# Moving the big loads of a decode kernel from SyncE's queue to GpSimd's, each as one packet

## The chip, the cores and the metric

The kernel runs on one core of one Trainium2 chip. The time is the device time of the program in microseconds (us), the median of several runs. Besides TensorE (PE), VectorE (DVE), ScalarE (ACT), GpSimd (POOL) and SyncE (SP), the core has 16 DMA engines, which move data between the chip's memory (HBM) and the on-chip memory SBUF. An engine that issues a DMA only hands it over; the 16 DMA engines do the moving, and a semaphore is raised by 16 when all of them are done.

## The reference

One step of decoding: attention over a cache of keys and values, beside a small MLP, on 8 batch rows. All arrays are bf16.

```
xn  = layernorm(x)                                  # x [8, 1, 640]
q   = (layernorm(x) @ wq) as [8, 32 heads, 1, 128]
p   = softmax(q . k_cache * 128**-0.5)              # k_cache [8, 32, 4096, 128]
o   = p . v_cache                                   # v_cache [8, 32, 4096, 128]
out = x + o @ wo + (gelu(layernorm(xn) @ w1 + b1) @ w2 + b2)   # w1 [640, 1728]
```

Each of the two caches has 8 x 32 x 4096 x 128 elements of two bytes, 268 MB. Every element is used once. Together with the weights 552 MB are read.

## The kernel before

**Tiles.** The work on the cache is cut into 32 rounds (`NQ`), one for a group of eight heads of one batch row. A round's keys are 8 heads x 4096 keys x 128 elements. They lie as 128 partitions of 256 keys (`NKEY`), that is 128 rows of 64 KB, 8192 KB in all; 16 partitions hold one head. The values of a round have the same layout. SBUF has three slots of this size: KA and KB take the keys of even and odd rounds, VS the values. There is no room for a fourth, so a load waits until its slot has been read for the last time.

**A round.** Scores are made in two ways at once. Of a partition's 256 keys, 80 go through TensorE: it transposes them eight keys at a time (`pe_T`), ScalarE copies the transposes from PSUM to SBUF (`act_T`), TensorE multiplies them with the queries (`pe_QK`). The other 176 go through DVE in three chunks (`dve_chunk`): a multiply with the query, which writes into the key slot itself, an addition of the two halves, a sum. `dve_sel` folds TensorE's part to the head that a partition holds, `dve_max` finds the maximum, `act_exp` makes the probabilities, `pe_PV` runs 256 small matmuls over the values, and `pe_RS`, `dve_rinv`, `act_O` and `o_norm` divide by the sum. GpSimd's own work in a round is small: `qrep` repeats the query, `k_ready` writes one number when the keys have landed and so releases TensorE, `o_norm` multiplies 128 x 8 numbers.

**Order.** The kernel writes one list of steps with positions (`at(position, function, ...)`) and sorts it; round i stands at 100 i. Each step appends instructions to its engine's list, with waits for tickets (a semaphore and a count). An engine does its own list strictly in order. TensorE's, DVE's and ScalarE's lists are then folded into hardware loops (`_replay_pe`, `_replay_loop`); those of SP and GpSimd are written out in full (`_replay`).

**Loads.** SP issues nearly all of them, in this order: wq (into the value slot), K0, K1, V0, then K(i+1) and V(i) by turns, the MLP weights, V31, Wo. `load_k` (line 365) waits, for rounds 2 to 5, for the last transposes and the last DVE chunk of round i-2 (tickets `kt`, `km`), and from round 6 on for the exp of round i-2; `load_v` (line 380) waits for the `pe_PV` of round i-1 (ticket `pv`). The value load of round 30 is cut in two DMAs at key 192 (`V_CUT`, line 240), so that `pe_PV(30)` can begin with the first piece; in TensorE's loop the second piece's semaphore is counted by an extra one (`_late`), which `consts_pool` raises first.

**The end.** After K31 the key slot KA is free for w1, w2 and what is made of them (`load_mlp`, line 375; `zero_w2b`, `load_w2b`; `sel_pool`, two large copies by GpSimd; `widen`, line 517, eight small ones that wait for w1 and b1). b1 comes through ACT's queue (`load_b1`), behind ScalarE's copy of round 30's result. When the keys of round 31 have been read, Wo comes into KB (`load_wl`, `load_wn`, lines 396 and 403), and the last matmuls use it while it arrives in pieces.

Of the kernel before, what the change touches and what calls it, by code (L numbers as in the profile page):

```python
# [14 lines left out]
P = 128  # L15
# [177 lines left out]
def bass_parallel_sum__gqa_block_cached__mixer_channel_mlp__decode_kernel(  # L193
# [21 lines left out]
    NQ = NHQ * B  # L215
    DC = D // P
    FB = F // P
# [11 lines left out]
    NS = 2  # L229
    LOOP0, LOOPN = 2, 15  # L230
    KLATE = 6
    assert NKEY == 256 and NQ == 32
    SLOT = NKEY * DH
    KA, KB, VS = 0, 1, 2
# [1 line left out]
    RW = P // HW  # L236
    NL = 3
    WN_CUT = (0, 5 * CT, 7 * CT, 7 * CT + CT // 2, HS * CT)
    V_CUT = (0, 192, 256)

    def jp_of(i):
        return 80
# [6 lines left out]
    def kslot(i):  # L249
        return KA if i % 2 == 0 else KB  # L250
# [8 lines left out]
    with ExitStack() as es:  # L259
        sb = lambda name, shape, dt: es.enter_context(nc.sbuf_tensor(name, shape, dt))  # L260
        ps = lambda name, shape, dt: es.enter_context(nc.psum_tensor(name, shape, dt))
        sem = lambda name: es.enter_context(nc.semaphore(name))

        S_sb = sb("S_sb", [P, 3, SLOT], BF)
        tile = [S_sb[:, s, :].rearrange("p (j d) -> p j d", d=DH) for s in range(3)]
# [12 lines left out]
        w1_sb = scratch(DC * F, P, KA).rearrange("p (c n) -> p c n", c=DC)  # L278
        w2_sb = scratch(FB * D, P, KA).rearrange("p (c n) -> p c n", n=D)
# [69 lines left out]
        ld_vl = [_Dma(sem(f"ld_vl{q}")) for q in range(1, len(V_CUT) - 1)]  # L349
        ld_wl = [_Dma(sem(f"ld_wl{q}")) for q in range(2)]  # L350
        ld_wn = [_Dma(sem(f"ld_wn{q}")) for q in range(len(WN_CUT) - 1)]
        tk = {}
        prog = []

        def at(pos, fn, *a):
            prog.append((pos, len(prog), fn, a))

        def load(key, dma, dst, src, eng=None):
            tk[key] = dma.sig((eng or sp).dma_start(dst, src))

        def cache_src(cache, i):
            hq, b = divmod(i, B)
            return cache[b, hq * HS:(hq + 1) * HS].rearrange("h (p j) d -> (h p) j d", j=NKEY)

        def load_k(i):
            s = kslot(i)
            if i >= KLATE:
                sp.wait(tk[("exp", i - 2)])
            elif i >= 2:
                sp.wait(tk[("kt", i - 2)], tk[("km", i - 2)])  # L370
            elif s == KB:
                sp.wait(tk["qmm"])
            tk[("k", i)] = ld_s[s].sig(sp.dma_start(tile[s], cache_src(A_k_cache, i)))

        def load_mlp():
            sp.wait(tk[("kt", NQ - 2)], tk[("km", NQ - 2)])
            load("w1", ld_w1, w1_sb, B_w1.rearrange("(p c) f -> p c f", c=DC))
            load("w2a", ld_w2a, w2_sb, B_w2[0:FB * P, :].rearrange("(p c) n -> p c n", c=FB))
# [12 lines left out]

        def load_b1():
            act.wait(tk[("kt", NQ - 2)], tk[("km", NQ - 2)])
            load("b1", ld_b1, b1_sb, B_b1.rearrange("(o f) -> o f", o=1), act)

        def load_wl(q):
            sp.wait(tk[("kt", NQ - 1)], tk[("km", NQ - 1)])
            lo, hi = (0, HW) if q == 0 else (HW, HW + HS)
            tk[("wl", q)] = ld_wl[q].sig(sp.dma_start(
                woW_sb if q == 0 else woL_sb[:, 0, :],  # L400
                A_wo[lo * DH:hi * DH, :].rearrange("(p s) n -> p (s n)", p=P)))

        def load_wn(q):
            lo, hi = WN_CUT[q], WN_CUT[q + 1]
            n = HS * DH
            tk[("wn", q)] = ld_wn[q].sig(sp.dma_start(
                woL_sb[:, 1, lo * CN:hi * CN],
                A_wo[NL * n:(NL + 1) * n, :].rearrange("(p s) n -> p (s n)", p=P)[:, lo * CN:hi * CN]))

# [12 lines left out]
        def consts_pool():  # L422
            pool.iota(iota_h, [[-HP, HS]], base=0, channel_multiplier=1)
            pool.iota(iota_w, [[-RW, HW]], base=0, channel_multiplier=1)
            tk["iota"] = pool.sig(pool.iota(iota_i, [[1, P]], base=0, channel_multiplier=-1))
            for d, (ap, v) in zip([None] + ld_vl + [None] * 2, (
                    (zeros_sb, 0.0), (ones_sb[:, :], 1.0), (mx_sb[:, :], 0.0), (mb_sb[:, :], 0.0))):
                inst = pool.memset(ap, v)
                if d is not None:
                    inst.call[3] = (d.sem, 1)  # L430
            tk["consts"] = pool.sig(pool.memset(ones_f[:, :], 1.0))

        def sel_pool():
# [186 lines left out]
        def dve_chunk(i, c):  # L620
            s = i % 2
            lo, hi = chunks(i)[c]
            w = hi - lo
            kt = tile[kslot(i)][:, lo:hi, :]
            dve.wait(tk[("k", i)], tk[("qb", i)])
            t = dve.sig(dve.tensor_tensor(
                kt, kt, qbc_sb[:, s, :][:, None, :].to_broadcast([P, w, DH]), ALU.mult))
            tk[("ym", i)] = t
            dve.wait(t)
            t = dve.sig(dve.tensor_tensor(kt[:, :, 0:DH // 2], kt[:, :, 0:DH // 2], kt[:, :, DH // 2:DH], ALU.add))  # L630
            dve.wait(t, tk.get(("exp", i - 2)))
            tk[("km", i)] = dve.sig(dve.tensor_reduce(Sd_sb[:, s, lo:hi], kt[:, :, 0:DH // 2], AX.X, ALU.add))
# [311 lines left out]
```

## Time and profile before

| | us |
|---|---|
| median of 3 runs | 1281.46 (1281.36 to 1281.47) |
| span of the profiled execution | 1280.1 |
| DVE busy | 1101.6 (86%) |
| PE busy | 672.0 (52%) |
| ACT busy | 477.0 (37%) |
| POOL busy | 109.3 (9%) |
| DMA queue q1 (SP's) | 551.79 MB in 10736 packets, 99.7% of 16 engines' span |
| other queues | q8 and q14 (instructions) 13 packets, q10 (ACT's) 36 packets |

The span reaches from the first to the last instruction; the run's time has a little more around it. A DMA queue's share is the time that its packets took, summed over the 16 DMA engines and divided by 16 spans. "Us to landing" of an issue counts from the issuing instruction to the last semaphore update, so it holds the time that the load waited behind others. Nearly every instruction has line L111, the helper that emits it, so groups are told apart by tiles: `S_sb` is the three slots, `kr_sb` the number that `k_ready` writes, `PV_ps` the result of `pe_PV`. In a timeline a row gives the start, the duration, the engine (a q behind it: issue only), the operation, the tiles and the count; brackets give the idle time of the engine before it and what ended it. "issue" there means that the profile shows nothing it waited for.

### The profile page before, as it was taken

To read this page: it belongs to the slowest core of one execution; us is meant where nothing else is said; L and a number is where in the kernel's file an instruction comes from. 1 tells how busy PE (TensorE), PEld (TensorE's weight loads), DVE (VectorE), ACT (ScalarE), POOL (GpSimd) and SP (SyncE) were. 2 spreads that over 40 slices of the span, in tenths; PEclk is the share of its full clock that TensorE was granted. 3 is DMA by queue.
4 is the path that set the end of the run, shared out by engine and by line. 5 is a ranking of instruction groups with operands and counts; after the bars stand their busy time and mean duration, and the time that the engine had idled before them with its cause. 6 is when DMAs were issued, how large, how long until landed. Compare 5 with 4: busy or idle time off the path is not lost.

```text
span 1280.1 us, 34355 instructions
## 1 busy us (share of the span) xinstructions
PE 672.0 (52%) x13906; PEld 573.2 (45%) x13906; DVE 1101.6 (86%) x681; ACT 477.0 (37%) x906; POOL 109.3 (9%) x119
## 2 busy tenths in 40 slices
PE   1636555446645446545456554456454466464476
PEld 1435444335535345444345444345343355353465
DVE  1899999889888889888898888898888898888894
ACT  0524444233444233443234443234442334442331
POOL 0020010000000000000000000000000000000050
PEclk9755565565565556555555555556555656655665
DMA  9999999999999999999999999999999999999998
GB/s 419 427 433 431 432 430 432 442 432 430 430 442 428 432 432 436 436 430 432 432 442 430 430 432 438 432 430 434 436 436 430 432 430 442 432 428 434 432 440 367
DMA packets 10785, 551.99 MB, mean 431 GB/s; under 512 B 1242, under 2 KB 1523, under 8 KB 1812
## 3 DMA queue, kind: packets, MB, share of 16 engines
q1 hardware_dynamic: 10736, 551.79, 99.7%
q8 instruction: 9, 0.15, 0.0%
q10 hardware_dynamic: 36, 0.02, 0.0%
q14 instruction: 4, 0.03, 0.0%
HBM read 551.80 MB, written 0.01 MB: 431 GB/s over the span
## 4 chain that ended last, share of the span: by engine, by line
DMA 47%; DVE 37%; issue 11%; ACT 4%; DVEq 0%; SPq 0%; PE 0%
DMA S_sb<-in_A_k_cache_dram 45%; DVE S_sb L111 26%; DVE Sd_sb L111 8%; ACT P_sb L111 4%; DMA S_sb<-in_A_wo_dram 2%; DVE S_ps L111 1%; DVE mx_sb L111 1%; DVE mbT_sb L111 0%; DVE mxT_sb L111 0%; DVE ri_sb L111 0%; DVE NB_sb L111 0%; DVEq L109 0%; DVE mq_sb L111 0%; DVE mb_sb L111 0%; SPq L111 0%
## 5 line engine op out<-in xcount | busy, mean ns | idle before, releaser
L111 PE MATMUL TR_ps<-ident_bf,S_sb 128*128 128x128 bf16 (+1 forms) x2570 | 343.3, 280 | 353.5 <-POOL kr_sb L111 333.2
L111 DVE TENSOR_TENSOR S_sb<-S_sb,qbc_sb 128x7552 bf16<-128x7552 bf16 (+1 forms) x96 | 388.7, 4049 | 128.3 <-DMA S_sb<-in_A_k_cache_dram 128.0
L111 PEld LDWEIGHTS TR_ps<-ident_bf,S_sb 128*128 (+2 forms) x2570 | 245.7, 103 | 411.7 <-issue 338.5
L111 DVE TENSOR_REDUCE Sd_sb<-S_sb 128x59 f32<-128x3776 bf16 (+1 forms) x96 | 390.2, 4065 | 6.0
L111 ACT ACTIVATE KT_sb<-TR_ps 128x1024 bf16<-128x1024 bf16 x320 | 327.0, 1024 | 121.6 <-PE TR_ps L111 109.6
L111 PE MATMUL PV_ps<-P_sb,S_sb 128*128 128x8 bf16 x8192 | 224.0, 175 | 140.6 <-DMA S_sb<-in_A_v_cache_dram 137.9
L111 PEld LDWEIGHTS PV_ps<-P_sb,S_sb 128*128 128x128 bf16 x8192 | 221.3, 103 | 143.3 <-DMA S_sb<-in_A_v_cache_dram 140.5
L111 DVE TENSOR_TENSOR S_sb<-S_sb 128x3776 bf16<-128x3776 bf16 (+1 forms) x96 | 206.5, 2151 | 3.3
L111 ACT ACTIVATE P_sb<-Sd_sb,NB_sb 128x256 bf16<-128x256 f32 x256 | 126.3, 494 | 210.9 <-DVE NB_sb L111 210.9
L111 PE MATMUL S_ps<-qrep_sb,KT_sb 128*128 128x8 bf16 x2560 | 121.9, 177 | 50.9 <-ACT KT_sb L111 47.8
L111 ACT ACTIVATE oU_sb<-PV_ps 128x8 f32<-128x8 f32 x31 | 5.5, 178 | 375.8 <-PE PV_ps L111 375.8
L111 PEld LDWEIGHTS S_ps<-qrep_sb,KT_sb 128*128 128x128 bf16 x2560 | 91.7, 103 | 82.4 <-ACT KT_sb L111 41.1
L111 POOL TENSOR_TENSOR oT_sb<-oU_sb,ri_sb 128x8 bf16<-128x8 f32 x31 | 71.8, 2315 | 370.8 <-DVE S_sb L111 315.3
L111 POOL COPY qrep_sb<-qT_sb 128x128 bf16<-128x128 bf16 x32 | 18.3, 573 | 474.7 <-PE S_ps L111 455.1
L111 ACT ACTIVATION_READ_ACCUMULATOR P_sb<-Sd_sb,NB_sb 128x1 f32 x256 | 47.8, 187 | 0.0
L111 DVE TENSOR_TENSOR S_ps<-S_ps,mask_sb 128x320 f32<-128x320 f32 (+1 forms) x65 | 31.6, 486 | 2.7 <-PE S_ps L111 2.7
L111 DVE TENSOR_REDUCE Sd_sb<-S_ps 128x40 f32<-128x320 f32 x64 | 31.5, 492 | 2.2
L111 PE MATMUL QB_ps<-ident_bf,qrep_sb 128*128 128x128 bf16 x32 | 9.1, 285 | 40.7 <-DVE S_sb L111 22.1
L111 ACT ACTIVATE qbc_sb<-QB_ps 128x128 bf16<-128x128 f32 x32 | 8.9, 278 | 57.6 <-PE QB_ps L111 57.6
L111 POOL MEMSET kr_sb<- 128x1 f32 x32 | 3.2, 99 | 294.9 <-DMA S_sb<-in_A_k_cache_dram 294.9
L111 PEld LDWEIGHTS QB_ps<-ident_bf,qrep_sb 128*128 128x128 bf16 x32 | 3.3, 103 | 43.6 <-ACT oU_sb L111 29.0
L111 PE MATMUL CH_ps<-rs_sb,ones_f 128*128 128x8 f32 x64 | 15.4, 313 | 6.5 <-ACT P_sb L111 6.5
(68 smaller groups left out, 150.6 us busy)
## 6 DMA issues: line engine op xcount, KB each, us to landing
S_sb<-in_A_v_cache_dram SPq DMA_DIRECT2D x1, 6144.0 KB, 26.8
S_sb<-in_A_wq_dram SPq DMA_DIRECT2D x1, 5120.0 KB, 15.6
S_sb<-in_A_wo_dram SPq DMA_DIRECT2D x1, 2560.0 KB, 18.4
S_sb<-in_B_w_dram SPq DMA_DIRECT2D x1, 2160.0 KB, 30.3
S_sb<-in_B_w_dram SPq DMA_DIRECT2D x1, 2080.0 KB, 34.9
S_sb<-in_A_v_cache_dram SPq DMA_DIRECT2D x1, 2048.0 KB, 31.4
S_sb<-in_A_wo_dram SPq DMA_DIRECT2D x1, 1280.0 KB, 21.1
S_sb<-in_A_wo_dram SPq DMA_DIRECT2D x1, 800.0 KB, 22.6
```

Of the source, the lines that this page charges most:

```text
L111: inst = getattr(e, name)(*a, **k)
```

## The change

- K2 to K31 and all V loads, the MLP weights w1 and w2 (except w2's last rows) and all of Wo are issued by GpSimd. wq, K0, K1 and w2's last rows stay with SP. GpSimd's list holds the issues between its other steps, so an issue also stands behind those.
- Each of these K and V loads has `single_packet`: the eight rows that a DMA engine moves for it are one packet instead of eight.
- V30 is one DMA: `V_CUT` has no inner cut, so `ld_vl` is empty and the extra counts go.
- The loads by GpSimd have semaphores of their own (`ld_g`).
- V0 waits, besides for the query matmuls, for the multiply of DVE's second chunk of round 0 (`ym0`).
- In the list, K(i) from round 2 on stands right behind `k_ready(i-1)` (100 i - 101) instead of behind `qrep(i)` (100 i - 51), and `load_mlp` just ahead of `k_ready(31)`. The tickets that they wait for are the same.

```diff
+    PACKET = {"single_packet": True}
...
-    V_CUT = (0, 192, 256)
+    V_CUT = (0, 256)
...
+        ld_g = [_Dma(sem(f"ld_g{s}")) for s in range(3)]
...
         def load_k(i):
             s = kslot(i)
+            if i < 2:
+                if s == KB:
+                    sp.wait(tk["qmm"])
+                tk[("k", i)] = ld_s[s].sig(sp.dma_start(tile[s], cache_src(A_k_cache, i)))
+                return
             if i >= KLATE:
-                sp.wait(tk[("exp", i - 2)])
-            elif i >= 2:
-                sp.wait(tk[("kt", i - 2)], tk[("km", i - 2)])
-            elif s == KB:
-                sp.wait(tk["qmm"])
-            tk[("k", i)] = ld_s[s].sig(sp.dma_start(tile[s], cache_src(A_k_cache, i)))
+                pool.wait(tk[("exp", i - 2)])
+            else:
+                pool.wait(tk[("kt", i - 2)], tk[("km", i - 2)])
+            tk[("k", i)] = ld_g[s].sig(pool.dma_start(tile[s], cache_src(A_k_cache, i), **PACKET))
 
         def load_mlp():
-            sp.wait(tk[("kt", NQ - 2)], tk[("km", NQ - 2)])
+            pool.wait(tk[("kt", NQ - 2)], tk[("km", NQ - 2)])
...
         def load_v(i):
-            sp.wait(tk["qmm"] if i == 0 else tk[("pv", i - 1)])
-            if i != NQ - 2:
-                tk[("v", i)] = [ld_s[VS].sig(sp.dma_start(tile[VS], cache_src(A_v_cache, i)))]
-                return
-            tk[("v", i)] = []
-            for d, lo, hi in zip([ld_s[VS]] + ld_vl, V_CUT[:-1], V_CUT[1:]):
-                if lo:
-                    d.n += 1
-                tk[("v", i)].append(
-                    d.sig(sp.dma_start(tile[VS][:, lo:hi, :], cache_src(A_v_cache, i)[:, lo:hi, :])))
+            pool.wait(tk["qmm"], tk["ym0"]) if i == 0 else pool.wait(tk[("pv", i - 1)])
+            tk[("v", i)] = [ld_g[VS].sig(pool.dma_start(tile[VS], cache_src(A_v_cache, i), **PACKET))]
...
         def load_wl(q):
-            sp.wait(tk[("kt", NQ - 1)], tk[("km", NQ - 1)])
+            pool.wait(tk[("kt", NQ - 1)], tk[("km", NQ - 1)])
...
         dve_chunk:
             tk[("ym", i)] = t
+            if i == 0 and c == 1:
+                tk["ym0"] = t
...
-        at(NQ * Q - 55, load_mlp)
+        at(NQ * Q - 102.5, load_mlp)
...
-                at(o - 51, load_k, i)
+                at(o - 51 if i < 2 else o - 101, load_k, i)
```

More of the change, by code (lines that the diff above doesn't have):

```diff
@@ L366, in load_k @@
             s = kslot(i)
-            if i >= KLATE:
-                sp.wait(tk[("exp", i - 2)])
-            elif i >= 2:
-                sp.wait(tk[("kt", i - 2)], tk[("km", i - 2)])
-            elif s == KB:
-                sp.wait(tk["qmm"])
-            tk[("k", i)] = ld_s[s].sig(sp.dma_start(tile[s], cache_src(A_k_cache, i)))
+            if i < 2:
[3 more added lines that the diff above has]
+                return
+            if i >= KLATE:
+                pool.wait(tk[("exp", i - 2)])
+            else:
+                pool.wait(tk[("kt", i - 2)], tk[("km", i - 2)])
+            tk[("k", i)] = ld_g[s].sig(pool.dma_start(tile[s], cache_src(A_k_cache, i), **PACKET))
         def load_mlp():
-            sp.wait(tk[("kt", NQ - 2)], tk[("km", NQ - 2)])
-            load("w1", ld_w1, w1_sb, B_w1.rearrange("(p c) f -> p c f", c=DC))
-            load("w2a", ld_w2a, w2_sb, B_w2[0:FB * P, :].rearrange("(p c) n -> p c n", c=FB))
+            pool.wait(tk[("kt", NQ - 2)], tk[("km", NQ - 2)])
+            load("w1", ld_w1, w1_sb, B_w1.rearrange("(p c) f -> p c f", c=DC), pool)
+            load("w2a", ld_w2a, w2_sb, B_w2[0:FB * P, :].rearrange("(p c) n -> p c n", c=FB), pool)
         def load_v(i):
-            sp.wait(tk["qmm"] if i == 0 else tk[("pv", i - 1)])
-            if i != NQ - 2:
-                tk[("v", i)] = [ld_s[VS].sig(sp.dma_start(tile[VS], cache_src(A_v_cache, i)))]
-                return
-            tk[("v", i)] = []
-            for d, lo, hi in zip([ld_s[VS]] + ld_vl, V_CUT[:-1], V_CUT[1:]):
-                if lo:
-                    d.n += 1
-                tk[("v", i)].append(
-                    d.sig(sp.dma_start(tile[VS][:, lo:hi, :], cache_src(A_v_cache, i)[:, lo:hi, :])))
+            pool.wait(tk["qmm"], tk["ym0"]) if i == 0 else pool.wait(tk[("pv", i - 1)])
+            tk[("v", i)] = [ld_g[VS].sig(pool.dma_start(tile[VS], cache_src(A_v_cache, i), **PACKET))]
         def load_b1():
@@ L396, in load_wl @@
         def load_wl(q):
-            sp.wait(tk[("kt", NQ - 1)], tk[("km", NQ - 1)])
+            pool.wait(tk[("kt", NQ - 1)], tk[("km", NQ - 1)])
             lo, hi = (0, HW) if q == 0 else (HW, HW + HS)
-            tk[("wl", q)] = ld_wl[q].sig(sp.dma_start(
+            tk[("wl", q)] = ld_wl[q].sig(pool.dma_start(
                 woW_sb if q == 0 else woL_sb[:, 0, :],
@@ L405, in load_wn @@
             n = HS * DH
-            tk[("wn", q)] = ld_wn[q].sig(sp.dma_start(
+            tk[("wn", q)] = ld_wn[q].sig(pool.dma_start(
                 woL_sb[:, 1, lo * CN:hi * CN],
@@ L425, in consts_pool @@
             tk["iota"] = pool.sig(pool.iota(iota_i, [[1, P]], base=0, channel_multiplier=-1))
[L426 to L430, printed above, removed]
+            for ap, v in ((zeros_sb, 0.0), (ones_sb[:, :], 1.0), (mx_sb[:, :], 0.0), (mb_sb[:, :], 0.0)):
+                pool.memset(ap, v)
             tk["consts"] = pool.sig(pool.memset(ones_f[:, :], 1.0))
```

## The prediction

> **What bounds the kernel now.** I read the page first: the queues and the chain that ended last.
>
> ```profile
> span 1280.1 us, 34355 instructions
> ...
> q1 hardware_dynamic: 10736, 551.79, 99.7%
> q8 instruction: 9, 0.15, 0.0%
> ...
> DMA 47%; DVE 37%; issue 11%; ACT 4%; DVEq 0%; SPq 0%; PE 0%
> ```
>
> SP's queue (q1) keeps 16 DMA engines busy for 99.7% of the span. So this is a transfer of 552 MB with everything else beside it, and the chain's 37% for DVE is only the way by which one K slot comes free for the next load. The span is 1280.1 us, the median of the runs 1281.46: 1.4 us lie outside it, and I add all differences to the median. Second view: time windows, a long steady one and one in which only Wo moves (columns: stretch, its length, PE, PEld, DVE, ACT, POOL, granted PE clock, DMA share, GB/s). Third: GpSimd's timeline, where the `kr_sb` memset marks a K load's landing.
>
> ```profile
> 249.19:1178.06 928.87, 486.86 (x10056) 414.68 (x10056) 812.76 (x480) 353.64 (x672) 65.34 (x72) 0.55 1.00 433
> ...
> 1266.00:1276.00 10.00, 9.70 (x340) 9.34 (x341) 0.59 (x3) 0.00 (x0) 0.00 (x0) 0.50 0.98 413
> ```
> ```profile
> 249.19 0.10 POOL L111 MEMSET kr_sb<- 128x1 f32 x1 [9.88 <-DMA S_sb<-in_A_k_cache_dram]
> ...
> 1178.06 0.10 POOL L111 MEMSET kr_sb<- 128x1 f32 x1 [9.88 <-DMA S_sb<-in_A_k_cache_dram]
> ```
>
> Between these two landings lie 24 pairs of one K and one V load: 928.87 / 24 = 38.70 us a pair, 19.35 us a load of 8192 KB. A load is 128 rows of 64 KB, eight on each DMA engine, so a row takes 2.42 us. The DMA share is 1.00. How early are the loads issued? Fourth view, the DMA issues (us from issue to landing):
>
> ```profile
> S_sb<-in_A_k_cache_dram SPq DMA_DIRECT2D x32, 38.7
> S_sb<-in_A_v_cache_dram SPq DMA_DIRECT2D x31, 31.6
> ```
>
> A K load waits 38.7 - 19.35 = 19.3 us in the queue before it moves, a V load 12.2 us. These are the margins against a later issue in the steady loop.
>
> **The change, part by part.**
>
> *One packet instead of eight.* Thirty K loads (K2 to K31) and all 32 V loads: 62. In the Wo window the engines moved 413 GB/s in 0.98 of the time, 421 while busy, against 433 in the steady window. There go the four larger Wo loads, 4960 KB in 4 x 128 packets.
>
> ```profile
> S_sb<-in_A_wo_dram SPq DMA_DIRECT2D x1, 2560.0 KB, 18.4
> ...
> S_sb<-in_A_wo_dram SPq DMA_DIRECT2D x1, 1280.0 KB, 21.1
> S_sb<-in_A_wo_dram SPq DMA_DIRECT2D x1, 800.0 KB, 22.6
> ```
>
> The window's 4.13 MB took 9.80 busy us and would have taken 9.54 at 433 GB/s: 0.26 x 16 = 4.2 engine-us over some 450 packets, about 9 ns a packet (an estimate; the two-digit share allows 3 to 16). If that cost belongs to the packet, a load saves 7 x 9 = 63 ns and 62 loads save 3.9 us; if it belongs to the row, nothing. I take -3.9 us, bounds 0 and 62 x 7 x 16 ns = -6.9.
> The Trainium skill, "DMA: Bandwidth & Descriptors", section "Why small descriptors are slow", gives a packet some 3 cycles and finds merging worth it only up to 256 B; at its 850 MHz that would be 62 x 7 x 3.5 ns = 1.5 us, an estimate from that page.
>
> *Issue by GpSimd, steady loop.* No plain load by GpSimd is in this trace. The nearest rows are SP's issues (0.33 us each) and GpSimd's small operations, which take up to 4.17 us when a DVE multiply runs beside them (below). Two of these, 8 us, still fit under 12.2 and 19.3 us: cost nothing, cover the queued load ahead. Past 12.2 us each further us would cost 1 us a V load. K(i+1) now stands behind `k_ready(i)` and V(i+1) behind `qrep(i+2)`; K(i+1) is released at about that landing anyway (K's 38.7 is the pair's 38.70), and qrep has begun when pv releases the V load:
>
> ```profile
> 263.19 0.52 POOL L111 COPY qrep_sb<-qT_sb 128x128 bf16<-128x128 bf16 x1 [13.91 <-PE S_ps L111]
> ```
> ```profile
> 275.56 0.33 SPq L111 DMA_DIRECT2D S_sb<-in_A_v_cache_dram  x1
> ```
>
> MLP and Wo issues lie behind small GpSimd work and ahead of their turn on the queue: nothing, except at the end, below.
>
> *The start.* Here the packet's length matters. The first loads, with V0's landing (the maximum of the V loads' times), and TensorE's first pass through its loop:
>
> ```profile
> 21.25 0.43 SPq L111 DMA_DIRECT2D S_sb<-in_A_v_cache_dram  x1
> 68.64 0.33 SPq L111 DMA_DIRECT2D S_sb<-in_A_k_cache_dram  x1
> 84.70 0.33 SPq L111 DMA_DIRECT2D S_sb<-in_A_v_cache_dram  x1
> 102.87 0.33 SPq L111 DMA_DIRECT2D S_sb<-in_A_k_cache_dram  x1
> ```
> ```profile
> DMA to landing us min/median/max: 24.2/31.6/53.5
> ```
> ```profile
> 74.86 4.90 PE L111 MATMUL PV_ps<-P_sb,S_sb 128*128 128x8 bf16 x178
> 82.44 2.23 PE L111 MATMUL PV_ps<-P_sb,S_sb 128*128 128x8 bf16 x78 [2.68 <-issue]
> 98.22 0.29 PE L111 MATMUL QB_ps<-ident_bf,qrep_sb 128*128 128x128 bf16 x1 [13.55 <-issue]
> ```
> ```profile
> 70.11 4.17 POOL L111 COPY qrep_sb<-qT_sb 128x128 bf16<-128x128 bf16 x1 [14.51 <-PE S_ps L111]
> ```
>
> TensorE stops in the middle of PV(0) for 2.68 us and behind it for 13.55 us, and "issue" says that nothing the profile shows held it; q8 brings nine instruction packets of some 16 KB over the same DMA engines. I read both stops as waits for instructions not yet fetched, behind rows of 2.42 us each.
> The Trainium skill, "DMA: Bandwidth & Descriptors", section "Queues, rings and completion order", says that an engine changes between queues only at packet ends; the 2.68 us agree with one row.
> With the load as one packet such a fetch waits for up to 19.35 us instead of 2.42. Worked through: V0 lands at 21.25 + 53.5 = 74.75, K2 moves until 94.1. PV(0) stops at 79.8 and goes on when K2's packet has ended, about 95.5; it ends at 97.7 instead of 84.7. V1, released by it, starts at about 99 (1.5 us for the issue): 5 us with no load on the engines. The second stop needs more fetches. If the last finds V1's packet started, it ends with it at 118.5, and TensorE takes up K2 at about 120 instead of 98. Its transposes and scores took until PV(1) began:
>
> ```profile
> 121.20 6.98 PE L111 MATMUL PV_ps<-P_sb,S_sb 128*128 128x8 bf16 x256
> ...
> 128.20 0.33 SPq L111 DMA_DIRECT2D S_sb<-in_A_v_cache_dram  x1
> ```
>
> that is 23 us after 98.22, about 8 of them behind ScalarE's exp, which would be done by then: 15 to 23. PV(1) ends at 142 to 150, V2 starts 1.5 us later, and K3 has ended at 138: 5.5 to 13.5 us idle. In all 10.5 to 18.5; I take 14. Bounds: 0, if the fetches are served between a packet's rows or come early enough; 33 us, if one more fetch waits for a whole load. That V0 now waits for `ym0` costs nothing: the multiply ends at 50.05 and K1 is on the engines until 55.5.
>
> ```profile
> 45.97 4.08 DVE L111 TENSOR_TENSOR S_sb<-S_sb,qbc_sb 128x7552 bf16<-128x7552 bf16 x1
> ```
> ```profile
> 55.50 0.10 POOL L111 MEMSET kr_sb<- 128x1 f32 x1 [5.25 <-DMA S_sb<-in_A_k_cache_dram]
> ```
>
> *The end.* V30 whole:
>
> ```profile
> S_sb<-in_A_v_cache_dram SPq DMA_DIRECT2D x1, 2048.0 KB, 31.4
> ```
> ```profile
> S_sb<-in_B_w_dram SPq DMA_DIRECT2D x1, 2080.0 KB, 34.9
> ```
> ```profile
> 1204.45 0.80 SPq L111 DMA_DIRECT2D S_sb<-in_A_v_cache_dram  x2
> ...
> 1238.33 0.34 SPq L111 DMA_DIRECT2D S_sb<-in_A_v_cache_dram  x1
> ```
> ```profile
> 1211.37 0.43 SPq L111 DMA_DIRECT2D S_sb<-in_B_w_dram  x1
> ```
> ```profile
> 1243.12 3.90 POOL L111 TENSOR_TENSOR oT_sb<-oU_sb,ri_sb 128x8 bf16<-128x8 f32 x1 [14.65 <-DVE ri_sb L111]
> ```
> ```profile
> 1242.88 4.04 DVE L111 TENSOR_TENSOR S_sb<-S_sb,qbc_sb 128x7552 bf16<-128x7552 bf16 x1
> 1246.96 2.15 DVE L111 TENSOR_TENSOR S_sb<-S_sb 128x3776 bf16<-128x3776 bf16 x1
> ```
>
> V30's second piece lands at 1204.9 + 31.4 = 1236.3. A whole PV takes 6.98 us, so V31 is released at 1243.3 instead of 1238.3; the MLP loads end at 1211.37 + 34.9 = 1246.3. Cover 3.0 us. GpSimd's own operation issued at 1243.12 ended only after the DVE multiply, at 1247.02. If V31's issue is held like that, it starts at about 1249: 2.5 us idle, 4.5 with the second multiply. Bounds 0 and 4.5; I take 2.5.
> The b1 load on ACT's queue comes behind pv(30) too. If its one packet falls behind V31's, `widen`, and with it GpSimd's Wo issues, move to V31's landing at 1265, some 8 us more; it needs V31 to be on the engines within a microsecond or two of its issue, so I leave it out of the sum and in the range.
>
> **Sum:** 1281.46 - 3.9 + 14 + 2.5 = 1294.1 us.
>
> **Rivals.**
> *A, faster: instructions come in time.* A page fetched ahead or served between rows leaves the start as it is, and V31's issue fits in its 3 us: 1281.46 - 3.9 = 1277.6. For it: from 121.20 on PV(1) is one run of 256 matmuls, so later passes need none of this. Against it: the stops of 2.68 and 13.55. It decides if start and end together cost under 1.3 us.
> The Trainium skill, "Runtime: NRT & Kernel Launch", section "Instruction fetch mechanics", says that a page crossing is mostly hidden, which is this rival; the two stops here disagree.
> *B, no difference:* the 9 ns stay with the row and the start is unharmed: 1281.46 + 0 + 1.5 (half of V31's delay, rounded up) = 1283. For it: the same rows as 64 KB each; nothing in the trace separates row from packet.
> *C, slower in the steady loop:* GpSimd's queue leaves a pause between loads. Above 0.06 us a load (3.9 / 62) it eats the gain, from 0.1 us it decides for slower; at 0.2 us, 62 x 0.2 - 3.9 gives 1290. Against it: with a load always queued there is no reason for a pause; the trace has no such load to show.
>
> **How the numbers follow.** 0.2% is 2.6 us, about what a measurement of this kernel can tell from no change: 1278.9 to 1284.0 is the same. Forecast 0.47, with a range of its own of 1285 to 1313 (10.5 + 0 - 6.9 and 33 + 2.5 - 3.9 from the median); A 0.33, B 0.10, C 0.10. Slower 0.57, same 0.10, faster 0.33. The range 1276.9 to 1309 leaves out A's best end and the forecast's worst.
>
> **What would show it.** K landings in the steady loop 38.58 us apart instead of 38.70 show the packet's gain. TensorE's stops between 60 and 125 us longer than 2.68 and 13.55, V1 and V2 issued with no load queued, and DMA tenths under 9 in the second to fifth slice show the start; the same slices full show A. V31's transfer beginning after 1246 less the gain shows the end. Wrong would be a landing distance above 38.70, which is C.

## The result, and the profile after

The kernel after the change takes 1283.18 us (median, 1282.37 to 1284.13), beside 1281.45 us (1281.16 to 1282.34) for the kernel before on the same chip: a ratio of 1.0013, with a 95% interval of 1.0007 to 1.0019. That is 1.7 us more, inside the 0.2% that the prediction called no change. Its forecast was 1294.1 us, 10.9 us too high. The profiled execution has a span of 1281.7 us against 1280.1 before.

First the page of the kernel after: its span, its queues and the chain that ended last.

```profile
span 1281.7 us, 34317 instructions
...
q0 software_dynamic: 9824, 529.68, 95.6%
q1 hardware_dynamic: 512, 22.11, 4.1%
...
DMA 88%; DVE 9%; issue 2%; POOL 0%; PE 0%; DVEq 0%; SPq 0%
```

GpSimd's queue (q0) now carries 530 of the 552 MB, and both queues together fill 99.7% of the span, as SP's queue did alone. They list 10336 packets, 400 fewer than before (10736). Had the request made one packet of an engine's eight rows, 62 x 16 x 7 = 6944 would be missing. The 88% for DMA in the chain is the same K loads, reached by another way. Next GpSimd's timeline, where `kr_sb` marks a K load's landing: first the kernel before, the rows that the prediction does not show.

```profile
35.87 0.10 POOL L111 MEMSET kr_sb<- 128x1 f32 x1 [14.20 <-DMA S_sb<-in_A_k_cache_dram]
...
133.09 0.10 POOL L111 MEMSET kr_sb<- 128x1 f32 x1 [1.97 <-DMA S_sb<-in_A_k_cache_dram]
...
1216.78 0.10 POOL L111 MEMSET kr_sb<- 128x1 f32 x1 [9.89 <-DMA S_sb<-in_A_k_cache_dram]
```

Then the kernel after, with its issue of V0:

```profile
35.80 0.10 POOL L111 MEMSET kr_sb<- 128x1 f32 x1 [14.69 <-DMA S_sb<-in_A_k_cache_dram]
...
50.29 0.71 POOL L111 DMA_DIRECT2D S_sb<-in_A_v_cache_dram  x1 [0.16 <-issue]
...
57.91 0.10 POOL L111 MEMSET kr_sb<- 128x1 f32 x1 [6.80 <-DMA S_sb<-in_A_k_cache_dram]
...
134.63 0.10 POOL L111 MEMSET kr_sb<- 128x1 f32 x1 [3.59 <-DMA S_sb<-in_A_k_cache_dram]
...
250.73 0.10 POOL L111 MEMSET kr_sb<- 128x1 f32 x1 [9.89 <-DMA S_sb<-in_A_k_cache_dram]
...
1179.69 0.10 POOL L111 MEMSET kr_sb<- 128x1 f32 x1 [9.90 <-DMA S_sb<-in_A_k_cache_dram]
...
1218.40 0.10 POOL L111 MEMSET kr_sb<- 128x1 f32 x1 [4.45 <-DMA S_sb<-in_A_k_cache_dram]
```

- **Steady loop:** from 250.73 to 1179.69 are 24 pairs in 928.96 us, 38.707 us a pair; before it was 928.87, 38.703. Neither the packet nor the issuing engine moved anything there. That already rules out a gain per load and a pause per load.
- **Start:** K0 lands at the same time (35.80 and 35.87), K1 2.41 us later (57.91 against 55.50), K3 1.54 us later (134.63 against 133.09). K31 is then 1.62 us late. So by the landings nearly the whole difference is there by 135 us.

A landing is the last of 16 engines, though. The trace also keeps a record of each DMA packet (start, duration, size, queue). Behind a load's rows each engine writes four bytes that report it done, and the last of these 16 reports makes the landing. Averaged over the 16 engines, K3 is done only 0.41 us later than before (132.17 against 131.76) and K31 0.48 us later (1215.98 against 1215.50). The rest of the 1.54 us is a spread between the engines: one ends K3 at 134.12, the next at 133.1. K1's rows are not late at all, their last one ends at 55.00 as before (55.01): two of the 16 reports of K1 stand behind a row of V0 each and come at 57.11 and 57.48.

TensorE's two stops, in its timeline of the kernel after:

```profile
85.24 2.23 PE L111 MATMUL PV_ps<-P_sb,S_sb 128*128 128x8 bf16 x78 [3.73 <-issue]
100.88 0.28 PE L111 MATMUL QB_ps<-ident_bf,qrep_sb 128*128 128x128 bf16 x1 [13.41 <-issue]
```

They are 3.73 and 13.41 us, against 2.68 and 13.55 before. No stop waits for a whole load of 19.35 us. The end, in GpSimd's and TensorE's timelines of the kernel after:

```profile
1245.06 0.53 POOL L111 DMA_DIRECT2D S_sb<-in_A_v_cache_dram  x1 [14.98 <-PE PV_ps L111]
1245.60 3.03 POOL L111 TENSOR_TENSOR oT_sb<-oU_sb,ri_sb 128x8 bf16<-128x8 f32 x1
```
```profile
1237.76 7.00 PE L111 MATMUL PV_ps<-P_sb,S_sb 128*128 128x8 bf16 x256 [4.86 <-DMA S_sb<-in_A_v_cache_dram]
...
1267.29 7.00 PE L111 MATMUL PV_ps<-P_sb,S_sb 128*128 128x8 bf16 x256 [6.15 <-DMA S_sb<-in_A_v_cache_dram]
```

V31 is issued at 1245.06, 6.7 us later than before (1238.33), and the issue took 0.53 us. PV(31) starts 1.67 us later than before:

```profile
1265.62 7.00 PE L111 MATMUL PV_ps<-P_sb,S_sb 128*128 128x8 bf16 x256 [5.92 <-DMA S_sb<-in_A_v_cache_dram]
```

From K31's landing to PV(31) it is 48.89 us after and 48.84 before, although V31 was issued so much later. Again the landing shows the slowest engine only. In the packet records V31's first rows start 1.27 us later than before on average (1246.55 against 1245.28) and take 3.02 us instead of 2.42, and its last rows end 1.92 us later (1266.53 against 1264.61). Of these 1.92 us, 0.48 were there at K31, so 1.44 are lost between K31 and the end of V31. The experiments ask three things: what the packet request does, what the end costs, and what delays the landings at the start.

### The profile page after: what moved, and what is told of

Its sections match the earlier page's. It is cut to its first block, busy times and chain, and to the rows that moved or that the text cites. A ratio compares the mean times of both kernels' runs of the same rounds, so it can differ in the third digit from the quotient of the medians.

```text
span 1281.7 us, 34317 instructions
## 1 busy us (share of the span) xinstructions
PE 671.9 (52%) x13906; PEld 572.9 (45%) x13906; DVE 1101.7 (86%) x681; ACT 477.5 (37%) x906; POOL 129.2 (10%) x189
## 2 busy tenths in 40 slices
DMA packets 10385, 551.99 MB, mean 431 GB/s; under 512 B 1226, under 2 KB 1283, under 8 KB 1540
## 4 chain that ended last, share of the span: by engine, by line
DMA 88%; DVE 9%; issue 2%; POOL 0%; PE 0%; DVEq 0%; SPq 0%
DMA S_sb<-in_A_k_cache_dram 86%; DVE S_sb L111 6%; DVE Sd_sb L111 3%; DMA S_sb<-in_A_wo_dram 2%; DVE S_ps L111 0%; POOL kr_sb L111 0%; DVE mx_sb L111 0%; PE ACC_ps L111 0%; POOL S_sb L111 0%; DVE ri_sb L111 0%; DVE mbT_sb L111 0%; DVE mxT_sb L111 0%; DVEq L109 0%; SPq L111 0%; DVE mq_sb L111 0%
## 5 line engine op out<-in xcount | busy, mean ns | idle before, releaser
L111 POOL TENSOR_TENSOR oT_sb<-oU_sb,ri_sb 128x8 bf16<-128x8 f32 x31 | 55.3, 1782 | 4.8 <-DVE ri_sb L111 4.3
L111 POOL DMA_DIRECT2D S_sb<-in_A_v_cache_dram x32 | 17.1, 536 | 368.4 <-DVE S_sb L111 315.4
L111 DVE TENSOR_TENSOR S_ps<-S_ps,mask_sb 128x320 f32<-128x320 f32 (+1 forms) x65 | 31.6, 486 | 2.7 <-PE S_ps L111 2.7
## 6 DMA issues: line engine op xcount, KB each, us to landing
S_sb<-in_A_v_cache_dram POOLq DMA_DIRECT2D x32, 31.4
S_sb<-in_A_k_cache_dram POOLq DMA_DIRECT2D x30, 38.4
```

What stands on the lines that cost most here:

```text
L111: inst = getattr(e, name)(*a, **k)
```

## Experiments on the packet

**Loads alone.** A kernel of loads only. One part moves 128 rows of 4 KB at a time, with and without the request, from SP and from GpSimd. The other part queues two loads of 8192 KB and sends small ones beside them from another engine.

```diff
+for e, packet in ((sp, False), (sp, True), (pool, False), (pool, True)):
+    ...  # 32 loads of 128 rows of 4 KB, then wait for all
+for e, other, packet in ((sp, act, False), (sp, act, True), (pool, sp, False), (pool, sp, True)):
+    ...  # two loads of 8192 KB by e, six of 64 KB by other, one after the other
```

> This kernel computes nothing of the reference; it only measures loads. First four stretches of 32 loads, each of 128 rows of 4 KB: issued by SP, by SP as one packet, by GpSimd, by GpSimd as one packet. Then four pairs of loads of 128 rows of 64 KB with six small loads one after the other beside them from another queue: SP without and with one packet (small loads from ACT), GpSimd without and with (small loads from SP). Theory 1 (the one-packet request does not change what a DMA engine does, on either queue): the stretches of one queue last the same with and without it, within 1%, and a small load beside the big ones takes the same 3 to 8 us with and without. Theory 2 (a packet is one unit and cheaper): the one-packet stretches are some 5% shorter (7 x 9 ns of some 8 x 160 ns), and small loads beside the one-packet loads take up to 19 us each. Theory 3 (SP's queue ignores the request, GpSimd's obeys): only the GpSimd pairs differ so.

In the timeline of this kernel, the first issues of the second, third and fourth stretch of 4 KB rows, and the first issues of the part with 64 KB rows; each stretch began when the one ahead had landed, the first at 0.74:

```profile
44.38 7.80 SPq L39 DMA_DIRECT2D S_sb<-in_A_k_cache_dram  x15
```
```profile
88.56 2.74 POOL L39 DMA_DIRECT2D S_sb<-in_A_k_cache_dram  x5 [88.12 <-DMA S_sb<-in_A_k_cache_dram]
```
```profile
132.83 1.57 POOL L39 DMA_DIRECT2D S_sb<-in_A_k_cache_dram  x3 [27.52 <-DMA S_sb<-in_A_k_cache_dram]
```
```profile
177.20 0.80 SPq L52 DMA_DIRECT2D S_sb<-in_A_k_cache_dram  x2
177.20 0.37 ACTq L55 DMA_DIRECT2D t_sb<-in_A_k_cache_dram  x1
```

The stretches took 43.64 us (SP), 44.18 (SP, one packet), 44.27 (GpSimd) and 44.37 (GpSimd, one packet): the request brings no gain (1.2% more on SP's queue, 0.2% on GpSimd's), even with rows of 4 KB, where seven packets' 9 ns would have been some 5% of a load's 1.37 us. The small loads beside the big ones, in the view of their tile:

```profile
DMA to landing us min/median/max: 1.8/1.9/23.5
```

A small load alone lands 1.9 us after its issue. Beside big loads of SP two landed after 22.4 and 19.5 us without the request and 22.1 and 19.6 with it; beside GpSimd's, 23.4 and 17.3 without and 23.5 and 17.3 with it. That is far above the 3 to 8 us that theory 1 expected, but the same with and without. The small load has eight rows on each engine, and 8 x 2.42 = 19.4 us: each of its rows waits for one row of 64 KB. A load that waited once for a whole load of 19.35 us would land at about the same time, so the packet records decide: beside the big loads the 16 engines start one small row each every 2.44 us (from 331.18, 333.62, 336.05 us and so on beside GpSimd's loads with the request), in all four pairs. So with the request, too, an engine changes between queues at every row.
The Trainium skill, "DMA: Bandwidth & Descriptors", section "Queues, rings and completion order", has an engine drain a whole packet before it turns to another queue. The runs do not contradict that as long as a packet is one row here; they show that the request did not make eight rows one packet.

**The change without the request.**

```diff
-    PACKET = {"single_packet": True}
+    PACKET = {}
```

> The changed kernel without the one-packet request, all loads still by GpSimd. Theory 1 (the request does nothing): 1283.2 us as the changed kernel, landings 38.71 us apart, TensorE's two stops at the start near 3 and 13.5 us. Theory 2 (the request gains some 4 us and something else loses 5.5): 1287, landings 38.77 apart. Theory 3 (the request costs at the start, as the prediction had it, only less): 1281.5 to 1282.

1283.2 us, ratio to the kernel before 1.0013 (1.0004 to 1.0022): the time of the change. Its GpSimd and TensorE timelines:

```profile
57.91 0.10 POOL L111 MEMSET kr_sb<- 128x1 f32 x1 [6.71 <-DMA S_sb<-in_A_k_cache_dram]
...
133.77 0.10 POOL L111 MEMSET kr_sb<- 128x1 f32 x1 [2.64 <-DMA S_sb<-in_A_k_cache_dram]
...
1217.62 0.10 POOL L111 MEMSET kr_sb<- 128x1 f32 x1 [4.45 <-DMA S_sb<-in_A_k_cache_dram]
```
```profile
82.97 2.23 PE L111 MATMUL PV_ps<-P_sb,S_sb 128*128 128x8 bf16 x78 [1.60 <-issue]
98.38 0.29 PE L111 MATMUL QB_ps<-ident_bf,qrep_sb 128*128 128x128 bf16 x1 [13.18 <-issue]
```

K1 is late by the same 2.41 us; so that has nothing to do with packets. K31 is only 0.84 us late here, but PV(31) starts at 1267.28, as in the change: what the start didn't cost, the end did (below). The stops of 1.60, 2.68 and 3.73 us look like one phenomenon, with a spread about the length of a row.

**The request alone, on SP's queue.**

```diff
-            tk[("k", i)] = ld_s[s].sig(sp.dma_start(tile[s], cache_src(A_k_cache, i)))
+            tk[("k", i)] = ld_s[s].sig(sp.dma_start(tile[s], cache_src(A_k_cache, i), single_packet=i >= 2))
```

(and the same for all V loads but V30; the rest is the kernel before)

> The kernel before, all loads on SP's queue, with the one-packet request for K2 to K31 and for the V loads (V30's two pieces without). Theory 1 (the request does nothing): 1281.5 us, landings 38.70 apart. Theory 2 (it saves the cost of seven packets a load): 1277.6, landings 38.58 apart, or, if instruction fetches wait for whole packets, 1290 and more with TensorE's stops at the start of 10 us and more each.

1281.39 us, ratio 1.0 (0.9991 to 1.0009); TensorE's stops are 3.39 and 12.84 us, and K31 lands at 1216.94 (before: 1216.78). The request does nothing on either queue. What the change costs comes from GpSimd's issues or from V30.

## Experiments on the end

**V30 whole, with SP's queue.** The kernel before with V30 as one load, and without the extra count for its second piece:

```diff
-    V_CUT = (0, 192, 256)
+    V_CUT = (0, 256)
```

> The kernel before with V30 as one load, all on SP's queue. Theory A (the whole V30 releases V31 5 us later, at 1243.2, and the engines run dry for a moment before V31): V31's issue at 1243.1 to 1243.4, 1282.2 to 1283.0 us. Theory B (the end is covered, the loss is at the start): V31's issue the same, the time 1281.4 to 1281.7.

1281.48 us, ratio 1.0 (0.9991 to 1.0009). SP's and TensorE's timelines:

```profile
1243.15 0.34 SPq L111 DMA_DIRECT2D S_sb<-in_A_v_cache_dram  x1
```
```profile
1265.53 6.99 PE L111 MATMUL PV_ps<-P_sb,S_sb 128*128 128x8 bf16 x256 [0.97 <-DMA S_sb<-in_A_v_cache_dram]
```

V31 is issued 4.8 us later than before, and PV(31) starts 0.09 us earlier. The MLP loads were still on the engines: the cover of 3.0 us that the prediction worked out (1243.3 against 1246.3) was enough.

**The change with V30 cut again.** `load_v` issues V30 in two pieces again, both by GpSimd, and a one-number write by GpSimd (`vr_sb`) tells TensorE that the second has landed:

```diff
-    V_CUT = (0, 256)
+    V_CUT = (0, 192, 256)
...
+        def v_ready():
+            for t, d in zip(tk[("v", NQ - 2)][1:], ld_vl):
+                pool.wait(t)
+                d.n += 1
+                d.sig(pool.memset(vr_sb[:, :], 0.0))
```

> The changed kernel with V30 cut at key 192 as before, both pieces by GpSimd; TensorE's wait for the second piece is raised by a small GpSimd memset behind that piece's landing. Theory A: V31 issued near 1240 instead of 1245.1, the engines stay fed, 1281.8 to 1282.2 us. Theory B: 1283.0 to 1283.3.

1282.70 us (1282.39 to 1283.64), ratio to before 1.0010 (1.0001 to 1.0019). GpSimd's and TensorE's timelines:

```profile
1217.78 0.10 POOL L111 MEMSET kr_sb<- 128x1 f32 x1 [4.45 <-DMA S_sb<-in_A_k_cache_dram]
...
1239.80 0.53 POOL L111 DMA_DIRECT2D S_sb<-in_A_v_cache_dram  x1 [2.24 <-PE PV_ps L111]
```
```profile
1266.75 7.00 PE L111 MATMUL PV_ps<-P_sb,S_sb 128*128 128x8 bf16 x256 [6.05 <-DMA S_sb<-in_A_v_cache_dram]
```

V31 is issued 5.3 us earlier than in the change, and about 0.5 us comes back (the intervals of the two kernels overlap). What the DMA engines did in that time, by windows from 1226 to 1256 us (the last two columns are DMA share and GB/s): before, after, and after with V30 cut.

```profile
1226.00:1256.00 30.00, 23.73 (x489) 21.21 (x486) 29.43 (x21) 7.98 (x14) 9.73 (x10) 0.61 1.02 439
```
```profile
1226.00:1256.00 30.00, 22.68 (x449) 20.95 (x448) 29.53 (x17) 8.19 (x10) 11.58 (x14) 0.50 0.96 403
```
```profile
1226.00:1256.00 30.00, 24.05 (x490) 21.98 (x489) 29.46 (x20) 7.67 (x11) 12.54 (x15) 0.54 1.01 433
```

403 against 433 GB/s is (433 - 403) x 30 / 433 = 2 us of transfer, to within a row of 2.42 us, as the window cuts rows. In the change the engines ran dry before V31 came; with V30 cut they did not. Here two things come together: K and V land 1 to 1.6 us late from the start, and PV(30) waits for the whole of V30, so it starts at 1237.76 instead of 1236.13, and V31's issue at 1245.06 lies 1.9 us behind the 1243.15 that SP's queue still covered. The packet records agree: V31's first rows take 2.42 us with V30 cut and 3.02 in the change, and the rows of V31 end 0.53 us later than before on average with V30 cut, 1.92 in the change. The slowest engine ends V31 1.12 us later than before with V30 cut (1266.24 against 1265.12), 1.78 in the change. So cutting V30 takes away most of what the engines lose at the end, but the engine that lags since the start is still late.

## Experiments on the start

**K0 and K1 by GpSimd as well.** If two queues meeting at K1 and V0 is what costs, one queue should not have it.

```diff
-                    sp.wait(tk["qmm"])
-                tk[("k", i)] = ld_s[s].sig(sp.dma_start(tile[s], cache_src(A_k_cache, i)))
+                    pool.wait(tk["qmm"])
+                tk[("k", i)] = ld_g[s].sig(pool.dma_start(tile[s], cache_src(A_k_cache, i), **PACKET))
...
-                at(o - 51 if i < 2 else o - 101, load_k, i)
+                at(-53 if i < 2 else o - 101, load_k, i)
```

> The changed kernel with K0 and K1 by GpSimd too, as one packet each, so that K1's and V0's rows stand in one queue. Theory A (the 1.5 us that are lost by the third K landing come from rows of two queues mixing on the DMA engines): K1 lands at 55.5 instead of 57.9, K3 at 133.1 to 133.9 instead of 134.6, and the time is 1281.7 to 1282.4. Theory B (a load by GpSimd starts or ends later by itself, whatever is beside it): K1 lands at 56.3 or later, K3 at 134.6 again, 1283.2.

1287.51 us, ratio 1.0046 (1.0033 to 1.006). The edit spoiled the experiment: wq stayed with SP, and now K0's rows shared the engines with it. The query matmuls came late, K1 was issued only at 37.63 (before, it was queued ahead), and from 20 to 50 us the engines moved 364 GB/s. It says nothing on the question, but it shows the price of letting a load that nobody waits for run beside one that is waited for.

**wq, K0 and K1 by GpSimd.**

```diff
-        at(-890, load, "wq", ld_wq, wq_sb, A_wq.rearrange("(p c) n -> p c n", c=DC))
+        at(-890, load, "wq", ld_wq, wq_sb, A_wq.rearrange("(p c) n -> p c n", c=DC), pool)
```

(beside the edits above)

> The changed kernel with wq, K0 and K1 by GpSimd too, so that all rows of the start stand in one queue (with K0 and K1 alone there, wq shared the engines with K0, landed late, and TensorE released K1 only at 37.6 us). Theory A (of the 1.75 us about 0.4 come from the place where SP's K1 and GpSimd's V0 meet, the rest from the end): K1 lands near 55.5, K3 0.4 to 1 us earlier than in the changed kernel relative to K0, and the time is 1282.6 to 1283.0. Theory B (all of the loss is at the start, as the K landings of the changed kernel say, 1.54 us by K3): 1281.5 to 1281.8.

1283.62 us (1282.53 to 1284.94), ratio 1.0016 (1.0007 to 1.0025). Its GpSimd timeline:

```profile
36.72 0.10 POOL L111 MEMSET kr_sb<- 128x1 f32 x1 [14.29 <-DMA S_sb<-in_A_k_cache_dram]
56.62 0.10 POOL L111 MEMSET kr_sb<- 128x1 f32 x1 [4.78 <-DMA S_sb<-in_A_k_cache_dram]
...
134.03 0.10 POOL L111 MEMSET kr_sb<- 128x1 f32 x1 [2.08 <-DMA S_sb<-in_A_k_cache_dram]
```

From K0 to K3 it is 97.31 us; before it was 133.09 - 35.87 = 97.22, in the change 98.83, and 97.88 and 98.20 in the change without the request and with V30 cut. In one queue the start costs 0.1 us instead of 0.7 to 1.6. The packet records show where that lies: the first row of V0 on each of the 16 engines takes 2.79 us on average in the change, 2.86 without the request and 2.98 with V30 cut, but 2.43 here and in the kernel before. That is 0.4 to 0.6 us on average, unequal over the engines (up to 3.9 us for one row); the spread does the rest. But K0 itself lands 0.9 us later, because the first load of the program moves later when GpSimd issues it, so nothing is won.

**The same with V30 cut.** Both of the edits above together.

> Both edits together: all loads by GpSimd from wq on, and V30 cut. If the place where the queues meet and the whole V30 are all of the loss, it gives the time of the kernel before, 1281.3 to 1281.8 us. If GpSimd's issues cost something of their own elsewhere, 1282 or more remain.

1283.63 us (1282.5 to 1284.56), ratio 1.0016 (1.0007 to 1.0025), where the parts added up would give some 1282.4 (before, and 0.9 for the first load). PV(31) starts at 1266.91, 1.29 us later than before, and the profiled span is 1281.4. The profiled execution itself took 1282.79, but the median is 0.84 above it: with all loads on GpSimd the executions scatter over more than 2 us, those of the kernel before over 1.2. In the packet records of that execution V31's rows end 0.87 us later than before on average, which is the delay of the first load and nothing more. The last 0.8 us lie in executions that no trace shows, and stay open.

**V0 only when K1 has landed.** The opposite edit: no sharing at all.

```diff
-            at(o + 50, load_v, i)
+            at(o + 50 if i else 98.5, load_v, i)
```

> The kernel after the change with V0's issue put behind k_ready(1), so that no row of V0 moves before K1 has landed. If sharing the engines with K1's last rows is what costs: K1 lands at 55.5 to 55.9 again, the engines then stand idle for 1.3 to 1.9 us (issue to first row), all engines alike, and K3 lands that much later than in the kernel before: 134.4 to 135.0, no better than after the change (134.63); TensorE's first stop in PV(0) moves by the same. If what costs is only that GpSimd's first rows come late, the same 134.4 to 135.0. If rows of two queues were what makes later loads late all the way, K3 to K31 would be 1083.7 apart again (1083.77 after, 1083.69 before) in each theory, and the end is as after the change: 1283 to 1284 in all. Faster than 1282.5 would say that sharing rows costs more than an idle of 1.3 us.

1286.25 us (1286.17 to 1286.36), ratio 1.0037 (1.0023 to 1.0051). Slower than each theory said. GpSimd's timeline, and the window from 50 to 60 us in the kernel before and in this one:

```profile
55.58 0.10 POOL L111 MEMSET kr_sb<- 128x1 f32 x1 [5.25 <-DMA S_sb<-in_A_k_cache_dram]
55.84 0.70 POOL L111 DMA_DIRECT2D S_sb<-in_A_v_cache_dram  x1 [0.16 <-issue]
...
137.63 0.10 POOL L111 MEMSET kr_sb<- 128x1 f32 x1 [6.42 <-DMA S_sb<-in_A_k_cache_dram]
```
```profile
50.00:60.00 10.00, 4.26 (x45) 3.25 (x45) 9.86 (x9) 2.59 (x4) 0.34 (x3) 0.50 0.98 426
```
```profile
50.00:60.00 10.00, 4.22 (x43) 3.10 (x43) 9.86 (x9) 2.42 (x4) 1.14 (x4) 0.52 0.57 216
```

K1 lands as before the change, but K3 comes 4.54 us later than before, not 1.3 to 1.9. The window lost (426 - 216) x 10 / 433 = 4.8 us of transfer. The expectation counted the idle time from K1's landing; but a load lands when the last of 16 engines is done, and in the records of the packets most engines had finished K1 some 2 us earlier, near 53.5, and V0's first rows moved from 57.3 on, taking 3.1 us instead of 2.42. So letting the rows share, as the change does, is the cheaper way by 3 us; that sharing as such is what costs is not borne out by this run.

**The meeting by itself.** Again loads only: one load of 8192 KB, and 14 us later two more by the same or by the other engine.

```diff
+for a, b in ((sp, sp), (sp, pool), (pool, sp), (pool, pool)):  # three times
+    a.dma_start(A_sb, ...)
+    ...  # 14 us of DVE work
+    b.dma_start(B_sb, ...); b.dma_start(C_sb, ...)
+    ...  # DVE writes fa_sb, fb_sb, fc_sb at the three landings
```

> Computes nothing of the reference: only loads, and some DVE work to set their times. Twelve rounds, three of each kind: a load of 8192 KB by one engine, 14 us later two more (8192 and 4096 KB) by a second engine; DVE writes one number at each landing. The kinds are SyncE then SyncE, SyncE then GpSimd, GpSimd then SyncE, GpSimd then GpSimd. 20 MB in all want 2.5 x 19.35 = 48.4 us behind the first row's start. Theory 1 (the meeting of the two engines' queues costs time of its own): in the two mixed kinds the first load lands about 2.4 us later than in its pure kind, because its last rows alternate with the second load's, and the third load lands 0.5 to 1.5 us later than in the pure kind of the same first engine, so that K3 1.5 us late after the change comes from there. Theory 2 (rows only change places): the first load lands 2.4 us later in the mixed kinds, the third one within 0.2 us of its pure kind; then K3's delay must come from when the loads are issued. Theory 3 (GpSimd's queue itself is slower): the third load lands late by the same amount in every kind where GpSimd issues it, SyncE before or not.

SP's and DVE's timelines of this kernel, the first round of SP alone and the first in which GpSimd issues behind SP:

```profile
2.86 0.40 SPq L41 DMA_DIRECT2D A_sb<-in_A_k_cache_dram  x1
...
54.02 0.33 SPq L41 DMA_DIRECT2D A_sb<-in_A_k_cache_dram  x1
```
```profile
24.91 0.06 DVE L51 MEMSET fa_sb<- 128x1 f32 x1 [7.91 <-DMA A_sb<-in_A_k_cache_dram]
...
53.93 0.06 DVE L51 MEMSET fc_sb<- 128x1 f32 x1 [9.65 <-DMA C_sb<-in_A_k_cache_dram]
80.83 0.06 DVE L51 MEMSET fa_sb<- 128x1 f32 x1 [12.67 <-DMA A_sb<-in_A_k_cache_dram]
...
105.06 0.06 DVE L51 MEMSET fc_sb<- 128x1 f32 x1 [9.64 <-DMA C_sb<-in_A_k_cache_dram]
```

| first, then | first load lands after | third load lands after (three rounds) |
|---|---|---|
| SP, SP | 22.0 us | 51.07, 50.97, 51.10 us |
| SP, GpSimd | 26.7 us | 51.04, 50.82, 50.95 us |
| GpSimd, SP | 27.0 us | 51.28, 51.00, 51.36 us |
| GpSimd, GpSimd | 22.2 us | 51.59, 51.31, 51.16 us |

The first load lands 4.7 us later when the second comes from the other engine: its last row and then its report, the four bytes behind the rows, each wait for a row of the other load. The last load lands when it did anyway, and no row is longer where the queues meet (2.42 us on average). So rows only change places, and the meeting by itself costs nothing: my theory that the queues' meeting takes time of its own falls. Where GpSimd issues the first load, the third lands 0.2 to 0.3 us later.

**The same beside DVE's multiplies.**

```diff
-                # 14 us of DVE work, then idle
+                # multiplies of 128x7552 from the first load's issue until 20 us behind the second engine's
```

> The twelve rounds of the run on meetings again (nothing of the reference is computed), but DVE multiplies tiles of 128x7552 from the first load's issue on until some 20 us behind the second engine's issue, as it does in round 0 when GpSimd issues V0. Theory 1 in its second form (the meeting costs time when DVE's multiplies run beside GpSimd's issue): the third load lands 0.4 to 1.5 us later than in the round of SyncE alone, 51.05 us after the first issue, where GpSimd issues behind SyncE, and GpSimd's issue rows are longer than 0.53 us. Theory 2 (rows only change places, DVE or not): 50.8 to 51.2 again in that kind, 51.0 to 51.6 in the two kinds that GpSimd begins, issue rows of 0.53 us; then the 0.45 to 1.5 us at the start come from something that only the whole kernel has.

GpSimd behind SP: 50.96, 50.81 and 50.95 us; SP alone 51.00, 51.75 and 50.90; SP behind GpSimd 51.12, 51.13 and 51.15; GpSimd behind GpSimd 51.31, 51.22 and 50.98; every GpSimd issue took 0.53 us but the first, 0.66. DVE's work does not make the meeting dear either.

## Why the prediction was wrong

The sum was -3.9 + 14 + 2.5 = 12.6 us; measured is +1.7.

- **The packet's gain, -3.9:** nothing. Landings are 38.707 us apart, not 38.58; the request alone gives 1281.39 against 1281.41. No packet of eight rows came about, so the runs put no price on a packet; whether the 9 ns worked out from the Wo window are the price of a row stays open. That nothing is gained was the other bound, and rival B's condition.
- **The fetch behind a whole packet, +14:** nothing. This is the step that failed. It took for granted that the request changes the unit at which a DMA engine changes between queues. The small loads beside big ones (22.4 and 22.1 us, 23.4 and 23.5) show, with their rows 2.44 us apart, that a row stays the unit. The first bound, 0, "if the fetches are served between a packet's rows", is what happened; the stops are 1.6 to 3.7 and 12.8 to 14.4 us in every run. Whether the request was passed over or does something else, no run shows. Nothing in the trace of before shows the unit for eight rows, but the chance of 0.47 leaned on the word packet and on no row.
The rule on packet ends of the Trainium skill, "DMA: Bandwidth & Descriptors", section "Queues, rings and completion order", which the prediction set beside the 2.68 us, was not wrong for rows; the prediction's use of it for eight rows was.
- **What it did not see at the start:** K1 lands 2.41 us late, since GpSimd's V0 comes on another queue and two engines move a row of it ahead of their report of K1. The prediction said that V0's issue "costs nothing" as K1 is on the engines until 55.5, and looked only at idle engines. Counted from K0's landing, K3 is then 0.7 to 1.6 us late in the three profiles where the queues meet there (the change, the change without the request, the change with V30 cut), and 0.1 with one queue. What is lost are the slow first rows of V0, 0.4 to 0.6 us averaged over the engines, and the spread that they leave. Why these rows are slow is not settled. The meeting alone, with loads only and with DVE at work, cost nothing. In the change V0 is GpSimd's first load and arrives just as K1's rows end; rows that start on idle engines are slow too (3.1 us with V0 behind K1's landing), but neither was separated from the other.
- **The end, +2.5:** the mechanism was half right, the size too large, the reason wrong. V31's rows begin at 1246.29, behind 1246 as the prediction's sign for the end has it, and averaged over the engines 1.44 us are lost there. But the issue was not held by a DVE multiply; at 1245.06 it took 0.53 us, while the `oT_sb` multiply behind it took 3.03. The cover was real: V30 whole costs nothing with SP's queue. But the start's delay ate it: V30 lands with its slowest engine and holds back PV(30) and V31's issue, while the other engines run dry. Cutting V30 again gives back about 0.5 us. Between K31's landing and PV(31) 0.4 to 0.8 us are added where the start was less late (49.66 us without the request, 49.22 with all loads on GpSimd, 48.84 before). In the change itself the landings do not show this piece, as the engine that lags at K31 is hardly later at the end of V31 (1.62 and 1.78 us) and the others fall back to it.
- **Steady loop, 0:** right. 62 issues by GpSimd moved nothing: V loads land 31.4 us after their issue (31.6 before), K loads 38.4 (38.7).
- **Rivals:** B gave 1283 and is nearest, and its two conditions held as far as the runs go (the request gains nothing, the start is not harmed by fetches). That its 1.5 us came out is partly chance: they were half of the delay that the prediction worked out for V31, from a cause that the runs do not bear out, and the runs find a second loss, at the start, that B did not have. A lacks its gain; C's pause did not come.

So the 1.7 us have no single place. Averaged over the engines, 0.48 us are lost at the start and 1.44 between K31 and the end of V31; by the slowest engine, which a landing waits for, 1.62 us are there at K31. The two do not add in the time, and taking away one of them leaves most of the loss: 1.2 us remain with V30 cut, and one queue loses as much at the first load as it wins. The packet records are of one execution of each kernel, and which engine lags differs between them. None of the versions beats the kernel before.

## What to carry to other kernels

An attribute that should change how a transfer is cut is tried alone in a small kernel of loads before anything is built on it: here the kernel of loads alone settles both the gain and the feared loss. When a load moves to another engine's queue, look at whom it overtakes: loads in one queue landed in order here, loads in two shared row by row, so that the one that is waited for landed later, although no engine idled. And a load's landing is the last of 16 engines: it can be 1.5 us late where the engines lost 0.4 us on average, and a successor that is issued only then finds most of them already idle.

## What the runs showed of the hardware that was not expected

- `single_packet` on plain loads brought no gain in time with rows of 4 KB or 64 KB, on SP's or on GpSimd's queue, and with rows of 64 KB the unit of sharing stayed the row.
- A 64 KB load beside a queued 8192 KB load on another queue lands after 17 to 23.5 us instead of 1.9.
- In the loads-only run two queues that meet share by rows without loss: the third load of three landed at 50.8 to 51.6 us in all four orders. Only the first load's landing moved, by 4.7 us; its report of four bytes, too, waits for a row of the other queue.
- The first 64 KB rows of a load took 3.1 us instead of 2.42 on idle engines (V0 behind K1's landing), 3.02 in V31 of the change and 2.8 to 3.0 in GpSimd's V0.
- An issue of a load by GpSimd takes 0.53 to 0.57 us on its timeline (0.66 to 0.71 the first time), beside a DVE multiply or not; by SP 0.33. The program's first load by GpSimd moved 0.9 us later than by SP.
